# Output stores one slot later, a causal ban on TensorE in two more blocks, both transposes of a batch together, and a separate tile for the tails: attention and a SiLU MLP on one core

## The chip, the cores and the metric

The kernel runs on one core of one Trainium2 chip. The metric is the device time of one execution in microseconds (us), as the median of several runs. Ratios are always computed as the mean time of one kernel's fast runs over the mean time of the other's fast runs in the same rounds on the same chip; that is not quite the ratio of the medians quoted beside it. "Same" means a difference within 2 %.

## The reference

```python
# attention with forgetting, 8 batches x 8 heads x 576 tokens x 64
scores = q @ k.T / 8                                # scale = 1/sqrt(64)
cum    = cumsum(log(clip(f, 1e-4, 1)))              # forget gates f in 0.8..1
scores = where(causal, scores + cum[:, None] - cum[None, :], -1e9)
attn   = softmax(scores) @ v
# MLP on the 4608 x 512 result
h   = x @ w_in                                      # 512 -> 2048
out = (h * sigmoid(h)) @ w_out                      # 2048 -> 512, float32
```

## The kernel before

The kernel orders the instructions of each engine by hand. It treats the first 128 tokens of each batch (the "first block", functions with a 0 in their names) apart from the other 448. The rest is done head pair by head pair: `NU` = 32 units `n`, which this document calls pairs 0 to 31. The MLP is cut into chunks: `m1_chunk` (`hp`, 4 matmuls of one slice of the hidden layer) and `m2_part` (`po`, 4 matmuls of the output). The attention's own matmuls are short and dependent, so MLP chunks are put between them as filler: `fill(us)` issues about so many us of ready chunks.

A pair gets its q and k in four steps: the SP queue loads them (`load_qk`), POOL casts them to bf16 into a tile `qkb` (`cast_qk`), the SP queue sends the DMA that transposes `qkb` into `qkT` (`transposes`), and TensorE multiplies (`scores`). I write T0, T1, ... for the transpose DMA of pair 0, 1, ...

```python
conv  = ctx.enter_context(tc.tile_pool(name="conv",  bufs=4))   # qkb, first blocks' and pairs'
opool = ctx.enter_context(tc.tile_pool(name="opool", bufs=3))   # osb, the outputs
# ... cut ...
def transposes(n):
    src = qbf.pop(n)
    t = qktp.tile([P, NX, P], BF16, name="qkT", tag="qkT")      # NX = 7
    qkT[n] = t[:, :, :].rearrange("p x c -> p (x c)")
    nc.sync.dma_start_transpose(out=t[:, :, :], in_=src[:, :, :].rearrange("p x c -> p (x c)"))
# ... cut: end of m2_part ...
        if done:
            osb = opool.tile([P, m1 - m0], FP32, name="osb", tag="osb")
            nc.scalar.activation(out=osb[:, :], in_=po[:, :], func=ACT.Copy, scale=0.5)
            for n, (r, b, s0) in enumerate(rows_of(g, tb)):
                t0 = b * S + s0
                q_ = nc.scalar if last and n == 1 else nc.sync
                q_.dma_start(out=out[t0 : t0 + r.stop - r.start, m0:m1], in_=osb[r, :])
# ... cut: first blocks 4..7, two at a time ...
    def two_more(b):
        for x in range(2):
            for i in range(2):
                turn0(b + x, i)                      # transpose q (i = 0), k (i = 1) on TensorE
                fill(0.3, 0, x == 1 or i == 1)
        scores0(b); mask0(b)                         # mask0: DVE multiplies by 0/1 after the exp
        fill(0.6, 2, 1)
        scores0(b + 1); mask0(b + 1)
        fill(2.4, 2, 3)
        # ... out0, back0 with fills between ...
# ... cut: the pairs ...
    def prepare(n):
        b, p = divmod(n, NP)
        if n + 4 < NU:
            load_qk(n + 4)
        if n + 2 < NU:
            cast_qk(n + 2)
            transposes(n + 2)
        # ... tails and v of the next batch ...
    for m in range(NQ):                              # two pairs each
        n = 2 * m
        piece = 1.3 if m < 2 else 2.4
        scores(n, 0); scores(n, 1)
        prepare(n);     slot(piece, 2)               # slot = fill, then new MLP groups become ready
        # ... back-transposes of the last two pairs ...
        scores(n, 2); scores(n + 1, 0)
        prepare(n + 1); slot(piece, 2)
        scores(n + 1, 1); scores(n + 1, 2)
        slot(piece, 2)
        attend(n); attend(n + 1)
        slot(min(3.5, max(0.8, behind() - LAG)) if m > 1 else 0.8, 1)
```

The block is shown with some short lines joined. The whole kernel:

The softmax here doesn't subtract the row's maximum and nothing guards it: scores larger than these inputs give would overflow.

## Time and profile before

The time is 361.01 us at the median of the first three runs (360.88 to 361.59).

The first line below is the page's list of busy times of before (busy us, share of the span, instructions). The second fence has the waits of TensorE between 27 and 100 us (engine, line, what it computes, what it waited for: us in all, times, longest).

```profile
PE 341.4 (96%) x3643; PEld 205.0 (57%) x3643; DVE 186.0 (52%) x410; ACT 218.8 (61%) x400; POOL 103.0 (29%) x183
```

```profile
PE sc L436 <- DMA qkT<-qkb: 3.5, 2, 2.7
PE sc L436 <- ACT u L440: 2.1, 3, 1.1
PE sc L305 <- DVE kT L278: 0.8, 1, 0.8
PE hp L535 <- ACT qkT L278: 0.7, 1, 0.7
PE hp L535 <- ACT x L367: 0.7, 1, 0.7
```

TensorE is by far the busiest engine, but the 96 % do not tell what can be won. Its waits and the spacing of its matmuls tell more. From 90 us to the end, the starts of the matmuls follow each other at their pitch, 0.86 us for four of 512 columns or 216 ns each (426 of the 476 distances after such a matmul are 215 or 216 ns). Before 90 us there are waits, and the list names them: pairs' scores wait for their transposed q and k and for the exp of an earlier score chunk, and the fifth and sixth first blocks wait for evacuations of their transposes.

Why are the transposes late? The next lines are from the SP queue's timeline of before (start, us that issuing took, queue, line, operation, out<-in, count), then one line of POOL's waits between 50 and 75 us, then TensorE's timeline where pair 4's scores start (in brackets the idle time before).

```profile
54.27 6.47 SPq L404 DMA_TRANSPOSE qkT<-qkb  x2
...
65.09 2.06 SPq L586 DMA_DIRECT2D out_dram<-osb  x3
...
69.72 1.26 SPq L404 DMA_TRANSPOSE qkT<-qkb  x1
...
79.03 0.55 SPq L586 DMA_DIRECT2D out_dram<-osb  x1
...
82.07 1.44 SPq L404 DMA_TRANSPOSE qkT<-qkb  x1
```

```profile
POOL qkb L376 <- DMA qkT<-qkb: 8.3, 1, 8.3
```

```profile
86.75 0.40 PE L436 MATMUL sc<-qkT 64*128 64x128 bf16 x8 [2.73 <-DMA qkT<-qkb]
```

T0 and T1 are the first line together: it spans 6.47 us because T1 had to wait. The POOL line says why: the cast for pair 1 waited 8.3 us until T0 had landed, because both casts had been given the same `qkb` buffer. T2 (69.72) and T4 (82.07) follow on the same queue, behind loads and output stores, and pair 4's scores then stand still for 2.73 us.

### The profile page before, as it was taken

Reading aid. Unit: us, or ns where it says so; the run is one execution under the profiler, and the core shown is the slowest. Engines: PE = TensorE matmul, PEld = TensorE weight load, DVE = VectorE, ACT = ScalarE, POOL = GpSimd, SP = SyncE. Lnnn points to the kernel's source line nnn. Section 1 sums busy time; section 2 is a strip of 40 time slices with the busy share of each in tenths; the row PEclk is TensorE's granted clock in tenths of the full one; section 3 lists DMA queues with packets and bytes.
Section 4 is the critical chain, followed back from the end, with each engine's and each line's share of the span. In section 5 each row is a group of like instructions: output and inputs, shape, how many; then the busy total and the mean of one; then the engine's idle time right before and its main releaser. Section 6 shows DMA issues by size and latency. Waiting matters only on the chain.

```text
span 356.9 us, 9037 instructions
## 1 busy us (share of the span) xinstructions
PE 341.4 (96%) x3643; PEld 205.0 (57%) x3643; DVE 186.0 (52%) x410; ACT 218.8 (61%) x400; POOL 103.0 (29%) x183
## 2 busy tenths in 40 slices
PE   8988999796999999999999999999999999999995
PEld 4643665455756566555665656756656565555564
DVE  4665854253556656454565555565655653435340
ACT  5655743774775956758567585676956844454341
POOL 6992125427154052126116207116200000000000
PEclk9999999999999999999999999999999999999999
DMA  8999996889798578497786667589502000011012
GB/s 157 218 203 201 199 195 102 226 171 199 170 215 184 134 148 168 113 190 183 112 193 151 152 151 152 145 162 203 123 27 62 31 28 33 29 38 53 31 60 59
DMA packets 139001, 47.92 MB, mean 134 GB/s; under 512 B 128016, under 2 KB 134416, under 8 KB 138960
## 3 DMA queue, kind: packets, MB, share of 16 engines
q1 hardware_dynamic: 132272, 40.93, 54.7%
q0 software_dynamic: 6528, 6.29, 10.6%
q8 instruction: 28, 0.46, 0.6%
q10 hardware_dynamic: 160, 0.13, 0.1%
q14 instruction: 13, 0.11, 0.1%
HBM read 36.85 MB, written 9.44 MB: 130 GB/s over the span
## 4 chain that ended last, share of the span: by engine, by line
PE 87%; DMA 6%; DVE 1%; SPq 1%; ACT 1%; POOL 1%; issue 1%; POOLq 0%; ACTq 0%
PE po L573 35%; PE hp L535 32%; PE sc L436 6%; PE dn L481 4%; DMA qkb<-in_q_dram 3%; PE dn L490 2%; PE tp L271 2%; PE tx L511 2%; PE wm L225 2%; DMA qkT<-qkb 1%; DMA vf<-in_v_dram 1%; DMA qf<-in_q_dram 1%; SPq L150 1%; PE sc L305 1%; SPq L404 1%
## 5 line engine op out<-in xcount | busy, mean ns | idle before, releaser
L543 ACT ACTIVATE th<-hp 128x384 bf16<-128x384 f32 (+2 forms) x208 | 95.4, 474 | 84.7 <-PE hp L535 82.0
L535 PE MATMUL hp<-x,w_in_bf 128*128 128x384 bf16 (+2 forms) x832 | 145.3, 314 | 1.6 <-ACT qkT L278 0.7
L573 PE MATMUL po<-w_out_bf,gt 128*128 128x512 bf16 (+1 forms) x592 | 146.5, 374 | 0.0
L544 DVE SCALAR_TENSOR_TENSOR gt<-th,hp 128x384 bf16<-128x384 bf16 (+2 forms) x208 | 106.0, 522 | 77.6 <-ACT th L543 75.2
L535 PEld LDWEIGHTS <-w_in_bf 128*128 128x128 bf16 x832 | 79.3, 98 | 54.4 <-issue 1.8
L440 ACT ACTIVATE u<-sc 128x1024 bf16<-128x1024 f32 (+1 forms) x96 | 74.2, 814 | 14.1 <-PE sc L436 13.9
L573 PEld LDWEIGHTS <-gt 128*128 128x128 bf16 x592 | 54.0, 98 | 48.9 <-issue 3.0
L390 POOL TENSOR_TENSOR vp<-vf,w_bf 128x520 bf16<-128x520 f32 (+1 forms) x32 | 34.3, 1073 | 54.2 <-DMA vf<-in_v_dram 52.3
L445 DVE TENSOR_TENSOR u<-u,tri 128x768 bf16<-128x768 bf16 x32 | 19.5, 611 | 30.1 <-ACT u L440 30.1
L436 PE MATMUL sc<-qkT 64*128 64x128 bf16 (+1 forms) x640 | 26.7, 207 | 5.6 <-DMA qkT<-qkb 3.5
L582 ACT ACTIVATE osb<-po 128x512 f32<-128x512 f32 (+1 forms) x37 | 21.9, 592 | 15.5 <-PE po L573 13.7
L376 POOL CAST qkb<-qf 128x384 bf16<-128x384 f32 x32 | 16.5, 515 | 47.0 <-DMA qf<-in_q_dram 34.0
L436 PEld LDWEIGHTS <-qkT 64*128 64x128 bf16 x640 | 18.4, 94 | 14.7 <-issue 7.7
L459 DVE TENSOR_TENSOR ut<-ut,trit 128x128 bf16<-128x128 bf16 x32 | 7.8, 243 | 30.2 <-ACT ut L452 30.0
L452 ACT ACTIVATE ut<-sc 128x640 bf16<-128x640 f32 x32 | 22.8, 712 | 0.0
L481 PEld LDWEIGHTS <-u 128*128 128x128 bf16 x576 | 20.6, 97 | 2.8 <-issue 0.2
L481 PE MATMUL dn<-vp,u 128*128 128x65 bf16 x384 | 21.8, 193 | 0.0
L499 DVE TENSOR_TENSOR xr<-dn,rec 128x448 bf16<-128x448 f32 x32 | 20.0, 624 | 1.1
L376 POOL CAST qkb<-kf 128x384 bf16<-128x384 f32 x32 | 16.7, 521 | 12.0 <-DMA kf<-in_k_dram 11.7
L481 PE MATMUL dn<-v,u 128*128 128x65 bf16 x192 | 19.8, 193 | 0.0
L436 PE MATMUL sc<-qkT,kT 64*128 64x64 bf16 (+1 forms) x128 | 16.0, 258 | 0.5 <-ACT ut L452 0.5
L380 POOL CAST qkb<-qktf 128x128 bf16<-128x128 f32 x32 | 10.7, 334 | 18.6 <-DMA qktf<-in_k_dram 18.6
(64 smaller groups left out, 194.7 us busy)
## 6 DMA issues: line engine op xcount, KB each, us to landing
vf<-in_v_dram SPq DMA_DIRECT2D x32, 256.0 KB, 4.8
out_dram<-osb SPq DMA_DIRECT2D x32, 256.0 KB, 2.1
qf<-in_q_dram SPq DMA_DIRECT2D x64, 96.0 KB, 2.8
kf<-in_k_dram SPq DMA_DIRECT2D x64, 96.0 KB, 2.6
w_in_bf<-in_moe_w_in_dram POOLq DMA_DIRECT2D x4, 512.0 KB, 9.4
w_out_bf<-in_moe_w_out_dram POOLq DMA_DIRECT2D x4, 512.0 KB, 13.2
qkb<-in_q_dram POOLq DMA_DIRECT2D x8, 128.0 KB, 6.4
qkb<-in_k_dram POOLq DMA_DIRECT2D x8, 128.0 KB, 6.5
```

The costliest lines, as they stand in the source:

```text
L376: nc.gpsimd.tensor_copy(out=t2[:, c0 : c0 + NR, :].rearrange("p c x -> p (c x)"), in_=t[:, :, :, :].rearrange("p c h d -> p (c h d)"),)
L390: nc.gpsimd.tensor_tensor(out=vbf[b][r, c, :, :], in0=vst[b][c][r, :, :], in1=w_bf[r, c + 1, b * H : (b + 1) * H, None].to_broadcast([n, H ...
L436: nc.tensor.matmul(sc[:, i, o : o + q1 - q0], lhsT=kt, rhs=t[r, q0:q1], start=True, stop=True)
L440: nc.scalar.activation(out=u[:, :, c * SM : c * SM + w], in_=sc[:, :, 0:w], func=ACT.Exp, scale=scale)
L452: nc.scalar.activation(out=ut[:, :, 0:3:2, :].rearrange("p k i t -> p i k t"), in_=sc[:, :, T0 : T0 + (NM + 1) * ST].rearrange("p i (k t) ...
L481: nc.tensor.matmul(dn[:, i * NR + c - 1, :], lhsT=u[:, i, o : o + P], rhs=vals(kb, i), start=(kb == 0), stop=(kb == c),)
L499: nc.vector.tensor_tensor(out=xq[:, :, p % 2, :], in0=dn[:, :, 0:D], in1=rec[:, :, None].to_broadcast([P, NGR, D]), op=ALU.mult,)
L535: nc.tensor.matmul(hp[:, :], lhsT=w_in_bf[:, cc, fc * P : (fc + 1) * P], rhs=xg(g)[:, cc, :], start=(cc == 0), stop=(cc == NCC - 1),)
L543: nc.scalar.activation(out=th[:, :], in_=hp[:, :], func=ACT.Tanh, scale=0.5)
L544: nc.vector.scalar_tensor_tensor(out=gt[:, fc, :], in0=th[:, :], scalar=1.0, in1=hp[:, :], op0=ALU.add, op1=ALU.mult,)
L573: nc.tensor.matmul(po[:, :], lhsT=gt[:, fc, tb * P : (tb + 1) * P], rhs=w_out_bf[:, fc, m0:m1], start=(fc == 0), stop=(fc == NFC - 1),)
L582: nc.scalar.activation(out=osb[:, :], in_=po[:, :], func=ACT.Copy, scale=0.5)
```

## The change

Its intent is to keep TensorE at work before 90 us. An output store is no longer issued right behind the copy it waits for, but a slot later, and more output buffers hold the results meanwhile. In the first blocks 4 and 5, the causal mask becomes a "ban" added by TensorE into PSUM before the scores, in place of a DVE multiplication after the exp. The two transposes of a batch's first block run together, with filler after both. The tails of the batches get an `x` tile of their own. The rule that mixes the chunks also changes.

```diff
-    opool = ctx.enter_context(tc.tile_pool(name="opool", bufs=3))
+    opool = ctx.enter_context(tc.tile_pool(name="opool", bufs=5))
@@ def xg(g)
-            tag, bufs = {4 * P: ("x4", 1), 2 * P: ("x2", 2), RB: ("x3", 3)}[GW[g]]
+            tag, bufs = {4 * P: ("x4", 1), 2 * P: ("x2" if g < 3 else "xt", 2), RB: ("x3", 3)}[GW[g]]
@@ m2_part
+    stores: list = []
+    def store(n):
+        n = max(n, 0)
+        for q_, dst, src in stores[:n]:
+            q_.dma_start(out=dst, in_=src)
+        del stores[:n]
 ...
         if done:
+            store(len(stores) - 4)
 ...
-                q_.dma_start(out=out[t0 : t0 + r.stop - r.start, m0:m1], in_=osb[r, :])
+                stores.append((q_, out[t0 : t0 + r.stop - r.start, m0:m1], osb[r, :]))
@@ order of the M2 chunks: group 0 no longer interleaves two row tiles
-        if g == 0:
-            M2 += [(g, t2 + tb, part) for t2 in range(0, nt, 2) for part in range(4) for tb in range(2)]
-        else:
-            M2 += [(g, tb, part) for tb in range(nt) for part in range(4)]
+        M2 += [(g, tb, part) for tb in range(nt) for part in range(4)]
@@ step
-            if want == at["last"] and at["row"] >= 2:
+            if want == at["last"] and at["row"] >= 2 and abs(f1 - f2) < 0.25:
@@ two_more
-    def two_more(b):
+    def two_more(b, banned):
         for x in range(2):
-            for i in range(2):
-                turn0(b + x, i)
-                fill(0.3, 0, x == 1 or i == 1)
-        scores0(b)
-        mask0(b)
-        fill(0.6, 2, 1)
-        scores0(b + 1)
-        mask0(b + 1)
-        fill(2.4, 2, 3)
+            turn0(b + x, 0)
+            turn0(b + x, 1)
+            fill(0.6, 0, 1)
+        for x in range(2):
+            if banned:
+                scores0(b + x, ban0(b + x))
+            else:
+                scores0(b + x)
+                mask0(b + x)
+            fill(0.6 if x == 0 else 2.0, 2, 1 if x == 0 else 2)
@@
-    two_more(4)
+    two_more(4, True)
 ...
-    two_more(6)
+    two_more(6, False)
@@ slot
+        n = len(stores)
         fill(us_, first)
+        store(n)
@@ end: the stores left over are issued before and between the last steps (cut)
```

More of the change, by code (lines that the diff above doesn't have):

```diff
@@ L818 @@
         ready.update(x[1])
+    store(len(stores))
     while step() is not None:
-        pass
+        store(len(stores))
     assert at["m1"] == len(M1) and at["m2"] == len(M2)
```

## The prediction

> **What bounds the kernel.** The page has PE busy 96%. [...] From 90 us to the last matmul (353 us) they follow at their pitch: four 128x512 per 0.86 us, 216 ns each[...]. No wait is left there; the tail stays.
>
> PE idles only before 90 us. From 27 us on, the start-to-start gaps beyond the pitch come to about 10.8 us: 2.9 between 30.9 and 41.2 (waits for the evacuations of the fifth and sixth blocks' transposes), 0.4 at 53.4, 3.7 between 66.7 and 72.7 (scores wait for exp: filler ran out), 0.95 at 77.3 and 2.9 at 86.7 (scores wait for the DMA transpose of pair 4).
>
> **Why those transposes are late.** In the SP queue's timeline, pair 0's transpose goes out at 54.27, pair 1's only at 59.51: its cast waited 8.3 us (POOL waits) for pair 0's transpose to land, because both casts share one qkb buffer. Then SP issues nearly without pause, three output stores (2.1 us) ahead of pair 4's loads among it.
>
> **What the change moves** (built programs compared).
> 1. Pair 1's cast gets block 5's buffer, freed at about 28 us. Its transpose can follow at about 55.6: 3.9 us earlier.
> 2. The stores move behind pair 2's transpose: another 2.1 us for it. Together pair 2's goes 69.7 -> about 63, pair 4's 82.1 -> about 75.
> 3. Ban for two blocks: 4 matmuls of 226 ns, +0.9 us of PE; takes two masks (0.7 us each) off DVE. Paired transposes (1.02 us for 32 instead of 2 x 0.57) save about 0.4 us and remove most of the waits at 30.9 to 41.2; I expect 0.6 us of new ones near 36 to 40.
> 4. 0.86 us fillers between the first two pairs' score chunks use the exp waits at 66.7 to 72.7.
> 5. Five osb buffers, separate x for tails: no wait shows their lack; worth nothing.
>
> **On the critical path.** The changed order reaches pair 0's scores about 56.4, but its transpose lands at 57.7 as now: new wait about 1.2. I add 0.3 for pair 1's transpose, 0.7 for an exp, 1.5 for pair 3's and 1.0 for pair 4's transpose. New idle in all about 5.3 us against 10.8; the ban less the pairing costs 0.5; longer rows of hp may cost 0.3 to 0.5 later. Pair 4's scores start at about 78.5 instead of 86.75 (-8.3), with 3 hp and 3 po chunks (3.9 us) left: net 4 us.
>
> **Prediction:** 357.0 us (-1.1%), range 354.3 to 360.4. Chances: faster by over 2% 0.07, within 2% 0.92, slower 0.01.
>
> **What would show it.** SP timeline: pair 1's transpose at about 55.6 without an 8 us POOL wait; pair 4's at about 75. PE: no exp waits of 0.5 to 1.2 us at pairs 0 and 1; a wait of about 1 us before pair 0's scores; no gaps beyond 90 us; about 5 us of idle from 27 to 90.
>
> **What would make it wrong.** If closer-packed loads saturate the DMA engines (share was 0.73 to 0.87 from 50 to 80 us, 1.17 after), the transposes land later and the gain goes to 0. If they land before PE arrives, the gain reaches 7 us. Long hp rows could wait for ACT.

## The result, and the profile after

After: 359.84 us at the median of 6 runs (358.79 to 360.24); before, in the same rounds, 360.87 us (360.15 to 361.59, 6 runs). The ratio is 0.997, with a 95 % interval of 0.9952 to 0.9988. So the change is a little faster, by about 1 us where 4 us were forecast, and counts as the same within 2 %. A second measurement on another chip gave a ratio of 0.9981 (0.9955 to 1.0007; it is the fifth experiment below).

Here are the same views after: TensorE's waits between 27 and 100 us, the SP queue, POOL's waits for `qkb` between 50 and 75 us, and TensorE at pair 3's and pair 4's scores.

```profile
PE sc L436 <- DMA qkT<-qkb: 4.0, 2, 2.8
PE tp L271 <- DMA qkb<-in_q_dram: 1.5, 1, 1.5
PE hp L535 <- DVE gt L544: 0.8, 1, 0.8
PE sc L436 <- ACT u L440: 0.5, 1, 0.5
```

```profile
54.77 2.87 SPq L404 DMA_TRANSPOSE qkT<-qkb  x2
...
64.12 1.26 SPq L404 DMA_TRANSPOSE qkT<-qkb  x1
65.42 1.07 SPq L559 DMA_DIRECT2D out_dram<-osb  x2
...
68.88 1.90 SPq L404 DMA_TRANSPOSE qkT<-qkb  x1
...
74.12 0.62 SPq L559 DMA_DIRECT2D out_dram<-osb  x1
...
77.36 1.25 SPq L404 DMA_TRANSPOSE qkT<-qkb  x1
```

```profile
POOL qkb L376 <- DMA kf<-in_k_dram: 2.9, 2, 2.0
POOL qkb L376 <- DMA qf<-in_q_dram: 1.2, 2, 0.8
```

```profile
72.90 0.40 PE L436 MATMUL sc<-qkT 64*128 64x128 bf16 x8 [2.77 <-DMA qkT<-qkb]
...
81.14 0.40 PE L436 MATMUL sc<-qkT 64*128 64x128 bf16 x8
```

What the reader is to see: the 8.3 us wait of POOL is gone, T0 and T1 go out back to back (2.87 us for both), and every later transpose is earlier. The waits for first-block evacuations and most of the exp waits are gone. But the total wait for transposed q and k did not fall; it was 3.5 us and is 4.0 us. It moved from pair 4 (86.75, 2.73 us) to pair 3 (72.90, 2.77 us). Pair 4's scores now start without a wait, at 81.14.

Behind the new wait something else appears. These lines are stretches of after with each engine's busy us (and instruction count), then the granted TensorE clock, the DMA share and the GB/s.

```profile
72.00:74.00 2.00, 1.10 (x12) 0.63 (x13) 0.00 (x0) 0.66 (x1) 0.00 (x0) 1.00 0.97 216
74.00:76.00 2.00, 2.00 (x22) 1.12 (x19) 0.88 (x2) 1.53 (x4) 1.57 (x2) 0.51 1.24 221
76.00:78.00 2.00, 2.00 (x18) 1.49 (x13) 0.36 (x2) 2.00 (x5) 2.00 (x5) 0.64 1.21 277
```

From 74.03 us TensorE ran at half clock for 3.41 us (the granted clock is 0.50 over 74.03 to 77.44; matmuls of 256 columns start 213 ns apart there, 109 elsewhere). The profiled execution of before had no such stretch until the last matmul was done (1.00 from 27 to 353 us), although its pair-4 wait was as long (2.73 us against 2.77).

To count idle time, take in each trace the start-to-start distance of successive matmuls beyond the pitch, and add it up by stretch. The pitch is the usual distance behind a matmul in the two traces at a clock of 1.00: 216 ns for 512 columns, 162.5 for 384, 109 for 256, 56 for 128, 29 to 30 for 65 and 29 for 64. The matmuls of 64 rows or 64 columns start in twos, 3 or 4 ns apart, and two such count as one. (TensorE's transposes are counted at 29 too, though their twos mostly start 56 ns apart; the rest is within the gaps, in before and after alike.) "Nominal" is the sum of the pitches (of the distances, where these are shorter). The slower matmuls of a half-clock stretch are within the gaps. The table is good to about 0.3 us.

| stretch, us | before | after | best (swap and filler, below) |
|---|---|---|---|
| up to 27 | 10.5 | 10.7 | 10.4 |
| 27 to 45 | 3.9 | 2.1 | 1.8 |
| 45 to 57 | 2.1 | 1.8 | 1.8 |
| 57 to 66 | 0.3 | 2.9 | 4.1 |
| 66 to 90 | 8.7 | 6.0 | 1.6 |
| 90 to 110 | 1.2 | 1.8 | 0.8 |
| from 110 | 8.8 | 9.5 | 9.1 |
| nominal matmul time | 316.25 | 316.88 | 316.92 |
| of the gaps from 27 to 90: those over 0.2 us | 10.7 | 6.2 | 4.0 |

Between 27 and 90 us the gaps fell from 15.0 to 12.9 us. The ban, less what the pairing of the transposes saves, costs 0.6 us of matmul time, the part beyond 90 us lost 1.3 us, and the start 0.2 us. In these two profiled executions it comes out even (the last matmul ends at 353.2 us in before and at 353.3 in after). The last row is what the prediction counted: it had 10.8 us for before and forecast about 5.3. To the 6.2 us measured, the half-clock stretch adds about 1.7 (an estimate: half of its 3.41 us), so 2.6 us more than forecast were lost there. The timed gain was 1 us, and the profiles hide it for a reason: the profiled execution of before took 358.71 us and was a lucky one, below all of that kernel's six timed runs and 2.2 us below their median, while that of after, 358.79 us, is only 1.1 us below the median of its own.

### The profile page after: what moved, and what is told of

Its sections match the earlier page's. It is cut to its first block, busy times and chain, and to the rows that moved or that the text cites. A ratio compares the mean times of both kernels' runs of the same rounds, so it can differ in the third digit from the quotient of the medians.

```text
span 357.0 us, 9042 instructions
## 1 busy us (share of the span) xinstructions
PE 343.6 (96%) x3647; PEld 205.6 (58%) x3647; DVE 182.9 (51%) x408; ACT 219.4 (61%) x400; POOL 102.5 (29%) x183
## 3 DMA queue, kind: packets, MB, share of 16 engines
q0 software_dynamic: 6528, 6.29, 10.7%
## 4 chain that ended last, share of the span: by engine, by line
PE 77%; DMA 12%; SPq 4%; issue 2%; POOL 2%; ACT 2%; DVE 1%; ACTq 0%; POOLq 0%
PE po L580 32%; PE hp L535 28%; PE sc L436 6%; DMA vf<-in_v_dram 5%; PE dn L481 4%; DMA w_out_bf<-in_moe_w_out_dram 4%; PE dn L490 2%; SPq L150 2%; PE tx L511 2%; DMA qktf<-in_k_dram 2%; PE wm L225 1%; DMA kf<-in_k_dram 1%; DMA qkT<-qkb 1%; POOL vp L390 1%; DVE gt L544 1%
## 5 line engine op out<-in xcount | busy, mean ns | idle before, releaser
L535 PE MATMUL hp<-x,w_in_bf 128*128 128x384 bf16 (+2 forms) x704 | 131.2, 323 | 1.1 <-DVE gt L544 0.8
L445 DVE TENSOR_TENSOR u<-u,tri 128x768 bf16<-128x768 bf16 x32 | 18.7, 585 | 31.0 <-ACT u L440 31.0
L376 POOL CAST qkb<-kf 128x384 bf16<-128x384 f32 x32 | 16.9, 529 | 10.7 <-DMA kf<-in_k_dram 10.4
L535 PE MATMUL hp<-xt,w_in_bf 128*128 128x256 bf16 x128 | 17.7, 273 | 0.0
```

What stands on the lines that cost most here:

```text
L376: nc.gpsimd.tensor_copy(out=t2[:, c0 : c0 + NR, :].rearrange("p c x -> p (c x)"), in_=t[:, :, :, :].rearrange("p c h d -> p (c h d)"),)
L535: nc.tensor.matmul(hp[:, :], lhsT=w_in_bf[:, cc, fc * P : (fc + 1) * P], rhs=xg(g)[:, cc, :], start=(cc == 0), stop=(cc == NCC - 1),)
```

## The experiments

The letters in the quoted expectations are working names of the theories; each quoted text is as it stood before the run. In words, the main theories were these. First, the pairing of the transposes acts through the buffer that pair 1's cast gets, and the store order is a small second term. Second (C in the texts), what ate the gain is the half-clock stretch behind pair 3's wait (the texts call such a stretch a window). Third (E), it is the order on the SP queue: `prepare` sends the loads for pair n+4 ahead of the transpose of pair n+2. Fourth (G), it is TensorE's filler, which was not moved along with the new DMA times: it stands behind pair 3's scores, and it is missing before them.

Runs share the runs of before on the same chip, which are given once: experiments 1 to 4 on one chip (before 360.27 us, 359.04 to 361.53, 11 runs), 5 to 8 on a second (360.80, 358.72 to 362.03, 11 runs), 9 to 12 on a third (359.95, 358.51 to 361.31, 11 runs). All outputs were correct.

### 1. Pairing alone

Before, with the two transposes of a batch together and nothing else:

```diff
         for x in range(2):
-            for i in range(2):
-                turn0(b + x, i)
-                fill(0.3, 0, x == 1 or i == 1)
+            turn0(b + x, 0)
+            turn0(b + x, 1)
+            fill(0.6, 0, 1)
```

> The kernel before with one part alone: both transposes of a block issued together (turn0, turn0, fill). The built program shows that this part alone gives pair 1's cast another buffer. Theory A (the buffer is what frees the DMA chain): pair 1's DMA transpose is issued within 2 us of pair 0's (before: 5.2 us), pair 3's lands about 3 us earlier than the 77.2 us of before, and the kernel is 0.5 to 2 us faster. Rival B (the stores in the SP queue are what mattered): time within 0.3 us of before.

Measured: 358.89 us (357.98 to 359.85), ratio 0.9959 (0.9935 to 0.9984). T1 is issued at 56.60 (before 59.51) and T4 at 78.70 (before 82.07). The 8.3 us wait of POOL for T0 is not in its trace. Of the waits between 30 and 42 us, three of 0.35, 0.35 and 0.26 us are left. New waits for transposes stand at pairs 2, 4 and 5 instead, the one at pair 2 (71.09) close to 3 us. TensorE's waits between 27 and 100 us:

```profile
PE sc L436 <- DMA qkT<-qkb: 4.4, 3, 2.9
```

So one edit, far from the pairs in the program, gives as much as the whole change within the intervals, and it frees T1 by the buffer that the pool hands out. In the built program of before, the casts of pairs 0 and 1 have the same address; with this edit pair 1's cast gets the buffer of a first block that was read at about 28 us. How much of the gain is T1's is not shown: the same edit also took 1.6 us off TensorE's gaps over 0.2 us between 27 and 45 us (3.0 before, 1.4 here), and one more `qkb` buffer without the pairing was not tried.

### 2. Store order alone

Before, with the list of stores and five output buffers as in the change's diff, and nothing else.

> The kernel before with the stores issued a slot later and five osb buffers, nothing else. Theory A: pair 1's DMA transpose still waits for pair 0's (issued about 5 us after it), the stores' 2.1 us move behind pair 2's transpose, gain at most 0.5 to 1 us, or nothing where PE then waits at another place. Rival B: it gives most of the 1.0 us that the whole change gave.

Measured: 359.40 us (358.41 to 360.07), ratio 0.9971 (0.9947 to 0.9996). T2 goes out at 67.97 (1.75 us earlier) but T4 at 81.23, only 0.84 us earlier. The three stores that stood ahead of T2 are now between T2 and T3 (at 69.33, 1.49 us for the three), so they still stand ahead of T4; just one store, that of 79.03, moved behind it (82.59). POOL still waits for T0:

```profile
POOL qkb L376 <- DMA qkT<-qkb: 9.6, 1, 9.6
```

This is the first mis-sized term of the forecast: it took 2.1 us off T2 for the stores (measured 1.75) and carried all of it on to T4, where they are worth 0.84.

### 3. The change without the pairing

After, with `two_more`'s first loop as in before (the reverse of the diff of experiment 1).

> The changed kernel with the transposes of a block apart again, all else kept; its built program gives pair 1's cast the shared buffer again. Theory A: pair 1's scores wait for its DMA transpose, 4 us and more of PE idle at about 60 to 64 us; slower than the changed kernel by 1 to 4 us, so at or above the time before. Rival B: same as the changed kernel within 0.5 us.

Measured: 363.69 us (363.16 to 365.07), ratio to before 1.0103 (1.0075 to 1.0131): clearly slower than before. T1 is back at 60.27, T4 at 81.30, two of the first-block waits are back (0.90 and 0.53 us), POOL waits for T0 again, and pair 3 now waits 3 us at a later time. The 4 us of idle expected at 60 to 64 us are a miss: the gaps there are 1.06 us before 62.87 and 1.01 before 64.10.

```profile
POOL qkb L376 <- DMA qkT<-qkb: 9.8, 1, 9.8
```

```profile
76.35 0.40 PE L436 MATMUL sc<-qkT 64*128 64x128 bf16 x8 [3.05 <-DMA qkT<-qkb]
```

The rest of the change depends on the pairing. My reading, argued and not tested apart, is that without it the ban's extra matmul time and the filler moved ahead are paid while the DMA chain that they were to bridge is as late as ever.

### 4. The change, with TensorE kept busy

After, with 12 matmuls on a constant in pair 3's wait, meant to keep the granted clock at 1.0 behind it:

```diff
         scores(n, 2)
+        if m == 1:
+            keep_warm(12)
         scores(n + 1, 0)
```

> The changed kernel with 12 useless 128x512 matmuls (2.6 us) put into the wait of 2.8 us before pair 3's scores; results unchanged. Theory C (that wait costs twice: it lets the granted clock drop to half for 3.4 us, which costs 1.7 us more): the clock stays at 1.0 in that stretch in all runs, and despite more work the kernel is 1 to 1.7 us faster than the changed kernel, about 358.3 us. Rival D (the drop of the clock lies in slack): same time as the changed kernel or slower by up to 0.5 us, though the clock stays up.

Measured: 361.07 us (359.64 to 361.94), ratio 1.0013 (0.9985 to 1.004), not better than after. In its trace (span 357.9 us) the half-clock stretch is gone (mean clock 0.999, in after 0.995) and pair 3 starts at 72.64, as the theory had it, but the next transposed pair, pair 4, makes TensorE wait:

```profile
69.94 2.76 PE L225 MATMUL wm<-warm 128*128 128x512 bf16 x12
72.64 0.40 PE L436 MATMUL sc<-qkT 64*128 64x128 bf16 x8
...
82.16 0.40 PE L436 MATMUL sc<-qkT 64*128 64x128 bf16 x8 [2.15 <-DMA qkT<-qkb]
```

T4 landed at 82.11, 1.07 us later than in after; but TensorE stood idle from 80.01, so it would have waited for a T4 at 81.04 too. So the half clock lay in slack: TensorE would have arrived at pair 4 that much earlier only to wait. The theory that the clock ate the gain falls as it was put. What limits this stretch is the landing of T4. Over whole runs, clock and time go together in some kernels and not in others. In this kernel's six runs the three with a mean clock of 0.999 or more took 359.64, 359.88 and 360.82 us, the three at 0.994 to 0.995 took 361.32, 361.43 and 361.94, a difference of the means of 1.45 us. In the changed kernel (the result's runs and those of experiment 5) it is the other way round: the three at 0.999 or more took 360.01, 360.77 and 360.84 us, the nine at 0.993 to 0.995 took 358.79 to 360.24. In before's runs there is no order either: on the third chip two runs at 1.0 took 359.18 and 359.51, and the four at 0.989 to 0.990 took 358.76 to 361.31.

### 5. The change again

> The changed kernel unaltered, as the yardstick on this chip for the three runs beside it. All theories: 0.995 to 0.999 of before. Granted clock in most runs about 0.994 (one window of 3.4 us at half clock after the wait for pair 3's DMA transpose), in the kernel before about 0.989 (two such windows).

Measured: 360.05 us (359.47 to 360.84), ratio 0.9981 (0.9955 to 1.0007). The profile repeats what the first one showed: T3 issued at 69.03 and landed at 72.88, pair 3 held up by 3.3 us, T4 landed at 81.52. It is the base for the next three on the same chip. Its waits for transposed q and k between 27 and 100 us:

```profile
PE sc L436 <- DMA qkT<-qkb: 4.4, 2, 3.1
```

### 6. The transposes issued ahead of the loads

After, with the order inside `prepare` swapped:

```diff
-        if n + 4 < NU:
-            load_qk(n + 4)
         if n + 2 < NU:
             cast_qk(n + 2)
             transposes(n + 2)
+        if n + 4 < NU:
+            load_qk(n + 4)
```

> The changed kernel with, in each step, the cast and DMA transpose of pair n+2 issued before the loads of pair n+4 instead of after them. Theory E (the SP queue's order of issue sets when the transposes land, and PE waits for those of pairs 3 and 4): transposes of pairs 2 to 4 issued about 2 us earlier each; the wait before pair 3's scores falls from 2.8 us to about 1; 1 to 2.5 us faster than the changed kernel. Rival F (DMA bandwidth or the landing of the loads that feed the casts sets it): the transposes are issued or land at the same times within 0.7 us; same time.

Measured: 357.54 us (357.27 to 359.01), ratio to before 0.9919 (0.989 to 0.9947). T2 goes out at 61.70 (in experiment 5: 64.31), T3 at 66.32 (69.03), T4 at 75.31 (77.85). T3 lands only 1.4 us earlier (71.49 against 72.88), since it took 5.2 us from issue to landing, so issue order is not all that sets it. Pair 3's hold-up falls from 3.3 to 1.7 us, and the trace has no half-clock stretch of 3.4 us (mean clock 0.998; in experiment 5: 0.995). The wait that is left for pair 4:

```profile
79.37 0.40 PE L436 MATMUL sc<-qkT 64*128 64x128 bf16 x8 [0.66 <-DMA qkT<-qkb]
```

The order on the SP queue is thus part of the cause, worth 2.5 us at the medians.

### 7. The filler moved to where TensorE waits

After, with the transposes left as late as they are, and MLP chunks issued earlier instead:

```diff
     two_more(6, False)
     ready.add(2)
+    fill(1.3, 0)
@@ for m in range(NQ)
         prepare(n)
-        slot(piece, 2)
+        slot(piece + (2.6 if m == 1 else 0.0), 2)
```

> The changed kernel with 1.3 us more of feed-forward work before pair 0's scores and 2.6 us more before pair 3's, taken from later. Theory G (PE wait that is left, about 1.4 us before pair 0 and 2.8 us before pair 3, is filler missing at that place): these two waits shrink to under 0.7 us together, part of it comes back as a wait for pair 4's transpose (2.3 us as in the kept-warm run); 1 to 3 us faster than the changed kernel. Rival (PE's waits there are all slack against the DMA chain of pairs 4 and 5): same time within 0.5 us.

Measured: 355.27 us (354.87 to 355.29, 4 runs), ratio 0.9844 (0.9814 to 0.9873). T3 and T4 land no earlier than in experiment 5 (73.79 and 81.91), and yet no wait over 0.3 us is left at pairs 3 and 4, nor the stall of 1 us at 98 us that after had. Only pair 0 waits, for a T0 that lands later here (60.03; in experiment 5: 58.55); that wait was to shrink and grew. TensorE's waits between 27 and 100 us, and the one at pair 0:

```profile
PE sc L436 <- DMA qkT<-qkb: 2.7, 1, 2.7
PE tp L271 <- DMA qkb<-in_k_dram: 0.2, 1, 0.2
```

```profile
60.08 0.45 PE L436 MATMUL sc<-qkT 64*128 64x128 bf16 x8 [2.67 <-DMA qkT<-qkb]
```

This is the strongest result. The transposes being late is only half of the cause; the other half is that the filler was in the wrong place. The count of matmuls shows it: pair 4's scores start no earlier than in experiment 5 (82.29 against 81.98), but 255.9 us of nominal matmul time are left from there on, against 259.8, so 3.9 us more work is done by then. Moving real work is worth 4.8 us at the medians; the same wait filled with matmuls on a constant (experiment 4) was worth nothing, because that work still had to be done later. The two fillers were moved together and not tested apart. This trace has a half-clock stretch too, from 60.29 us behind pair 0's wait (the granted clock is 0.57 in 60 to 62 us and in 62 to 64), and is faster all the same.

### 8. Both

After, with the edits of 6 and 7.

> Both of the two edits before. Theories E and G together: 3 to 5 us faster than the changed kernel, about 355 to 356.5 us, faster than both kernels, with at most 2 us of PE waits from 57 to 90 us. Rival: no better than the better one of the two alone.

Measured: 353.42 us (351.71 to 356.22), ratio 0.9799 (0.9761 to 0.9838) to before: faster than both kernels and the best median, though whether it is over 2 % faster than before is unclear by the interval, and its lead over experiment 7 is not clear of the intervals either. Its waits of TensorE between 27 and 100 us:

```profile
PE sc L436 <- DMA qkT<-qkb: 3.0, 1, 3.0
PE tp L271 <- DMA qkb<-in_k_dram: 0.2, 1, 0.2
PE dn L481 <- DVE gt L544: 0.2, 1, 0.2
```

The one of 3.0 us is pair 0's, so the 2 us at most that were expected between 57 and 90 us are a miss. Its six runs follow the clock: the four at 0.998 or more took 351.71 to 353.61 us, one at 0.995 took 354.45, one at 0.989 took 356.22.

### 9. Before again, for its clock

> The kernel before unaltered, for a trace of its usual run: nearly all its timed runs have a granted clock of 0.988 to 0.991, while the profile that the prediction was read from had 1.0. Theory C2: two windows of 3.4 us at half clock, each right behind one of its long waits (27 to 33 us, and 84 to 89 us), about 3.4 us of TensorE work lost in all, so that profile was a lucky run and the usual one has waits plus slow matmuls. Rival: the slow stretch lies in the start-up or behind the last matmul, where it costs nothing.

Measured: 360.45 us in a single run (state unknown), mean clock 0.99. TensorE's waits are those of the first profile to 0.4 us, but there are two half-clock stretches, from 69.85 and from 86.92 us, of about 3.4 us each by the clock in the view below and the mean of the run (the first was expected behind the waits at 27 to 33 us: a miss). In the stretches view:

```profile
69.00:71.00 2.00, 1.48 (x28) 1.19 (x28) 0.78 (x2) 2.00 (x4) 0.00 (x0) 0.71 1.03 244
71.00:73.00 2.00, 2.00 (x40) 2.00 (x38) 1.06 (x3) 0.62 (x2) 1.26 (x3) 0.50 0.85 175
73.00:75.00 2.00, 2.00 (x29) 1.11 (x27) 0.83 (x2) 0.52 (x2) 0.00 (x0) 0.93 0.81 182
86.00:88.00 2.00, 1.14 (x13) 0.67 (x14) 0.00 (x0) 0.51 (x1) 0.75 (x2) 0.73 0.92 198
88.00:90.00 2.00, 2.00 (x7) 0.84 (x6) 0.56 (x1) 1.43 (x2) 1.26 (x3) 0.50 1.15 249
```

So the first profile of before, with its mean clock of 1.000, was an exception: most of before's runs (23 of 33 on the three chips) have a mean clock of 0.988 to 0.991. The same wait for pair 4's transpose can thus be followed by half clock or not: in the first profile of before it lasted from 84.02 to 86.75 us and the clock stayed at 1.00, here the longest wait was 2.5 us and half clock starts at 86.92. In after the wait from 70.13 to 72.90 us was followed by half clock from 74.03. What decides it is not shown.

### 10. The change without the ban

```diff
-    two_more(4, True)
+    two_more(4, False)
```

> The changed kernel with the mask on VectorE again for the fifth and sixth blocks, all else kept. As predicted, the ban costs 0.9 us of TensorE time there; the waits at 30.9 to 41.2 us were removed by the pairing, not by the ban. If so: 28 to 41 us stays free of waits, PE arrives 0.5 to 0.9 us earlier at 41 us, but the kernel gains at most 0.5 us, because PE then waits that much longer for pair 0's transpose. Rival (the ban removed the waits): waits of 0.5 us and more come back at 30 to 34 us and the kernel is no faster.

Measured: 359.81 us (358.90 to 362.75), ratio 1.0009 (0.9973 to 1.0045). The nominal matmul time falls by 0.9 us as it should (316.0 against 316.9), and TensorE then waits longer for the transposes:

```profile
PE sc L436 <- DMA qkT<-qkb: 7.1, 3, 3.2
```

The gaps at 30.9 to 34 us stay away, so the pairing removed those, not the ban. But two gaps of 0.36 us stand at 36.5 and 38.0 us, which after does not have (experiment 1 has them too), so the ban took 0.7 us of waits away for its 0.9 us of matmuls. No gain from leaving it out is seen.

### 11. The best version, with T0 and T1 earlier

After, with the edits of experiment 8 and the first two transposes each right behind its cast:

```diff
+    cast_qk(0)
+    transposes(0)
     load_qk(2)
+    cast_qk(1)
+    transposes(1)
     load_v(0, 2)
     load_v(0, 3)
-    for n in range(2):
-        cast_qk(n)
-        transposes(n)
```

> The swap and the moved filler, and the DMA transposes of pairs 0 and 1 issued as soon as their casts are done, ahead of the loads of pair 2 and of the last two V chunks. Theory E again: pair 0's transpose is issued at about 51 us instead of 54.9, lands at about 54.5, and the wait of 3 us before pair 0's scores goes: 2 to 3 us faster than the run with swap and filler (0.980 of before), about 0.973. Rival (DMA bandwidth at 50 to 60 us sets it): the transpose lands at 58 us or later still, no gain.

Measured: 356.31 us (355.28 to 357.52), ratio 0.9911 (0.9878 to 0.9943). T0 goes out at 51.00 and lands at 55.27, and pair 0's wait is gone. But T2 now goes out at 64.91 (62.50 in experiment 8) and lands at 69.67 (65.83), and the wait stands at pair 2. The loads of v that were moved behind T0 and T1 are the likely reason, by the trace: POOL's conversion of v (`vp`) stood waiting for its loads until 61.23 us (57.71 in experiment 8), and the cast for pair 2, the next work on POOL, started at 63.48 (60.69):

```profile
POOL vp L390 <- DMA vf<-in_v_dram: 5.4, 1, 5.4
```

```profile
69.71 0.40 PE L436 MATMUL sc<-qkT 64*128 64x128 bf16 x8 [2.46 <-DMA qkT<-qkb]
```

A miss: the label says "best", and it is not. Compared by ratios, since the chips differ, experiment 8 (0.9799) stays ahead. All six runs here have a mean clock of 0.995, the figure of after's profiled execution with its one half-clock stretch.

### 12. The same without the ban

Experiment 11 with `two_more(4, False)`.

> The run before without the ban in the fifth and sixth blocks. With the DMA chain out of the way TensorE's own work counts, so leaving out 0.9 us of ban matmuls should now show: 0.5 to 0.9 us faster than with it. Rival: the masks on VectorE bring waits back that cost as much, same time.

Measured: 355.61 us (355.12 to 357.62), ratio 0.9899 (0.9867 to 0.9931). The difference from experiment 11 is inside both intervals, so the 0.5 to 0.9 us expected are not shown: inconclusive.

## Why the prediction was right or wrong

It named the direction and the mechanism, and missed the size: 357.0 us was forecast (354.3 to 360.4), 359.84 was measured, inside the range but with a quarter of the gain (1.0 of 4.0 us).

The transposes, issue and landing in us, show most of it:

| | T1 | T2 | T3 | T4 |
|---|---|---|---|---|
| before | 59.51, 63.49 | 69.72, 72.76 | 73.31, 77.24 | 82.07, 86.71 |
| forecast for after | 55.6 | about 63 | not given | about 75 |
| after | 56.41, 59.68 | 64.12, 67.10 | 68.88, 72.85 | 77.36, 81.04 |
| pairing alone | 56.60, 59.60 | 66.37, 71.04 | 71.09, 74.50 | 78.70, 82.33 |
| stores alone | 60.74, 63.65 | 67.97, 71.14 | 73.41, 77.02 | 81.23, 85.68 |
| best (experiment 8) | 56.56, 61.40 | 62.50, 65.83 | 67.09, 73.13 | 76.16, 80.05 |

**Step 1, pair 1's buffer: right.** The 8.3 us wait vanished and T1 came 3.1 us earlier (forecast 3.9). Experiments 1 to 3 show that the pairing alone decides when T1 goes out.

**Step 2, stores and the sum for pair 4: the step that failed.** The forecast had "another 2.1 us for it", and then moved T4 by 7.1 us, which is more than its two items, 3.9 and 2.1, give together. Pairing alone moved T4 by 3.4 us, stores alone by 0.84, both by 4.7. The stores did move behind T2, but two of them then stand between T2 and T4 (1.07 us of issuing at 65.42), and another at 74.12. From T2's issue to T4's the SP queue was issuing for 12.6 of 13.24 us in after (added from its timeline), so whatever is put ahead of T4 on that queue pushes it out: with the loads put behind it (experiment 6) it went out 2.5 us earlier, at 75.31. T4 went out at 77.36 where about 75 was forecast, and this term carried the 4 us.

**Pair 4's scores: forecast 78.5, measured 81.14.** This is the number on which the 4 us rested. T4's landing at 81.04 sets it: experiment 4 brought TensorE there earlier and it had to wait. So 5.6 us were won instead of 8.3 at this point, and 2.4 of the 2.6 us that are missing are T4's later issue. From what was won go, as the forecast reckoned, 3.9 us of MLP chunks that after has not yet done by then (by the count of matmuls, 259.8 us of nominal time are left in after and 255.9 in before). What is left is 1.7 us, and the gaps from there to the end are 1.8 us longer than in before, 1.3 of it beyond 90 us. So these two executions come out even; the timed gain of 1.0 us is about the difference between how far they lie below their medians (2.2 and 1.1 us).

**Pair 3's wait: forecast 1.5 us, measured 2.9 (3.3 in the repeat).** T3 took 4.0 us from issue to landing. The prediction names no time for T3, neither issue nor landing; T0 to T4 of before had taken 3.0 to 4.6. Pair 0's wait was right (1.2 forecast, 1.4 measured), and so were the waits for T1 or an exp (1.0 in sum, 1.0 measured). The wait forecast for pair 4 (1.0) did not appear: the wait at pair 3 and the half clock behind it came first and covered it.

**The half clock: not foreseen.** The wait of 2.73 us before pair 4 in before had no half-clock stretch behind it, the one of 2.77 us before pair 3 in after had; what decides it is not shown (experiment 9). It is not the cause of the lost gain here (experiment 4), but it makes the base less sure: the profile on which I had built was an execution of before without it.

**Beyond 90 us: forecast 0.3 to 0.5, measured 1.3 by the table.** The largest stall ends at 99.05 us and cost TensorE 1.0 us: it stands before the last of five chunks of `hp` in a row, while ACT did two exps before their activations. That the new mixing rule made the row is likely and not tested. Experiment 7 has no such stall at that place.

**Step 3, ban and pairing of the first blocks: right.** The ban cost 0.9 us (0.9 forecast) and nearly all of the waits between 30.9 and 41.2 us went. By experiment 10 the large ones went through the pairing, and two of 0.36 us through the ban.

**Steps 4 and 5: right.** The exp waits fell from 2.1 to 0.5 us, and no run shows a wait for an output buffer. The separate tail tile is needed for the order to build.

So where did the expected gain go? The change made T4 go out 4.7 us earlier, where 7.1 were forecast, and left the filler where it was. The wait moved from pair 4 to pair 3. Put the filler in front of pair 3 and the transposes ahead of the loads, and the changed kernel is 2 % faster than before instead of 0.3 % (experiment 8). Two things stay open: why T0 lands at 60.0 to 60.5 us in experiments 7 and 8 and at 58.6 to 58.9 in after, though it was issued at the same time; and how much of the 3 us wait at pair 0 in experiment 8 could be filled. Loads on another queue were not tried either. What they could win is not shown; issue time is what was short on the SP queue (12.6 of 13.24 us between T2 and T4).

## What to carry to other kernels

When a change makes one chain faster, retime the filler on the other engine with it: a wait only changes its place while the ready work still stands on the wrong side of it (here 2.73 us before pair 4 became 2.77 us before pair 3). Count, for each transfer that matters, everything issued ahead of it on its queue between the old position and the new, since work that is moved behind one transfer can still be ahead of the next (here three stores, 1.49 us of issuing, moved from ahead of T2 to between T2 and T3). And take a second look at the "before" profile for the clock of the execution it shows (here 1.000, where most runs have 0.988 to 0.991), before you build a sum of a few microseconds on it.
